# The K stage in pairs of d_ff tiles, its 64 remaining channels as two row tiles of TensorE

## The chip, the cores and the metric

The kernel runs on one core of a Trainium2 chip. The time is the device time of one execution in microseconds (us); lower is better. The granted TensorE clock was 0.998 to 1.0 in every profiled run, and every run quoted here is recorded as fast (none shows the lower clock and longer time of a slow run).

## The reference, cut to what matters

A causal convolution over 7 positions runs along the sequence, and its output goes through a channel mix. B = 8 batches, S = 4160 positions, D = 192 channels, d_ff = 1024.

```python
xk = mu_k * x + (1.0 - mu_k) * x_prev
xr = mu_r * x + (1.0 - mu_r) * x_prev
k = np.maximum(xk @ w_k, 0.0)          # K: 192 -> 1024
v = k * k @ w_v                        # V: 1024 -> 192
r = 1.0 / (1.0 + np.exp(-(xr @ w_r)))  # R: 192 -> 192
return (r * v).astype(np.float32)
```

192 channels are 128 and 64: the full height of TensorE's array of 128 rows, and half of it. The change is about that half.

## The kernel before: the parts that matter

Two batches are worked on together. For a step of 512 positions, `xk[:, 0, :]` and `xk[:, 1, :]` hold the 128 high channels of the two batches, and `xk[:, 2, :]` their 64 low channels, one batch on partitions 0 to 63 and the other on 64 to 127. The low matmul uses all 128 rows with weights of which one half is zeros.

```python
    def load_w(w, src):
        nc.gpsimd.dma_start(out=w[:, 0, :], in_=src[0:P, :])
        nc.gpsimd.dma_start(out=w[0:LO, 1, :], in_=src[P:D, :])
        nc.gpsimd.dma_start(out=w[LO:P, 2, :], in_=src[P:D, :])
        nc.gpsimd.memset(w[LO:P, 1, :], 0.0)
        nc.gpsimd.memset(w[0:LO, 2, :], 0.0)

    def load_rest():
        load_w(wr, moe_w_r)
        nc.gpsimd.dma_start(out=wv, in_=moe_w_v.rearrange("(f p) d -> p f d", p=P))
    # ... cut ...
    def k_mm(n):                      # one slot: one tile f of 128 d_ff channels
        # ... cut ...
            for i in range(2):        # L308
                nc.tensor.matmul(
                    out=ps[:, i, :], lhsT=wk[:, 0, fs], rhs=xk[:, i, :], start=True, stop=False
                )
            for i in range(2):        # L312
                nc.tensor.matmul(
                    out=ps[:, i, :], lhsT=wk[:, 1 + i, fs], rhs=xk[:, 2, :], start=False, stop=True
                )
```

The schedule is written by hand, slot by slot. A slot issues one K tile, then what a table has for it: R and V matmuls of an earlier step, and for later steps a convolution head (`conv_mm`) or a group of six transposes (`tr_mm`). ScalarE takes the Relu, the sigmoid and copies of the convolution (`conv_out`); VectorE takes squares, mixes, the product with R and the copies of the transposes (`tr_out`).

```python
            for h in range(H):
                at(pe, c0 + h, conv_mm, p, g, h)      # c0 = n0 - 22: eight slots in a row
                # ... cut: conv_out one slot later ...
            for j in range((nb + 1) // 2):
                at(pe, r0 + j, tr_mm, p, g, j)        # r0 = n0 - 13: five slots in a row
                at(dve, r0 + 1 + j, tr_out, p, g, j)
    # ... cut ...
        for n in range(-60, NSLOT + LAG_V + 3):
            run(early, n)
            if 0 <= n < NSLOT:
                k_mm(n)
            run(act, n)
            run(pe, n)
            if 0 <= n < NSLOT:
                k_relu(n)
            run(dve, n)
            if 1 <= n <= NSLOT:
                k_square(n - 1)
```

Three pools of PSUM, the memory that the matmuls write, hold two buffers each: for K (`psK`), for V, and one (`psM`) that convolution, transposes and R share in turn. A matmul into `psM` therefore waits until the tile before the last one has been copied out.

## Time and profile before

| | before |
|---|---|
| time, median of 4 runs (range) | 523.50 us (523.03 to 525.36) |
| span of the profiled run | 519.7 us |
| busy: TensorE, VectorE, ScalarE | 95%, 82%, 73% |
| TensorE's share of the chain that ended last | 92% |
| K matmul of 512 columns, start to start | 216 ns |

The prediction below shows the lines. Busy time counts records that overlap on TensorE, so the cost of a matmul is the distance between two starts, not its mean duration. The chain says which engine sets the end: here TensorE, in all its stages. The profiled run took 521.39 us, less than each of the four timed ones; e9 below has the likely cause, the start.

### The profile page before, as it was taken

The numbers are of one execution on the slowest core, as the hardware profiler recorded it, in microseconds if no ns is written. First come the engines' busy times: TensorE is split into PE (matmuls) and PEld (weight loads), VectorE is DVE, ScalarE is ACT, GpSimd is POOL, SyncE is SP. The second block draws the span as 40 slices with busy tenths as digits, with TensorE's granted clock in tenths as the row PEclk, the third lists the DMA queues.
The fourth block names the chain that finished last, engine by engine and source line by source line (L and its number), as shares of the span: only waits on it lengthen the run. The fifth ranks groups of instructions, "written<-read, shape, count | busy, mean of one in ns | idle before, by whom it ended". The sixth has DMA issues, their size and how long they took to land.

```text
span 519.7 us, 10640 instructions
## 1 busy us (share of the span) xinstructions
PE 492.5 (95%) x4256; PEld 360.1 (69%) x4256; DVE 425.3 (82%) x676; ACT 380.0 (73%) x545; POOL 51.9 (10%) x74
## 2 busy tenths in 40 slices
PE   0597999999999999999999999999999999999996
PEld 0345777777777777777777777777777777777776
DVE  1498897979889797997889799797898979798862
ACT  3278768687787868778686877868687786867772
POOL 9532100001020000101002010100100000000000
PEclk9999999999999999999999999999999999999999
DMA  9986451818136181714517171451711111121113
GB/s 126 171 94 85 72 106 47 130 47 129 48 71 113 47 130 47 115 62 74 101 62 115 55 115 62 76 101 52 123 47 62 56 47 62 47 62 62 49 58 100
DMA packets 76625, 41.92 MB, mean 81 GB/s; under 512 B 42912, under 2 KB 76192, under 8 KB 76576
## 3 DMA queue, kind: packets, MB, share of 16 engines
q0 software_dynamic: 39184, 15.15, 25.7%
q1 hardware_dynamic: 37392, 26.10, 16.6%
q8 instruction: 33, 0.54, 0.4%
q14 instruction: 16, 0.13, 0.1%
HBM read 30.56 MB, written 25.82 MB: 108 GB/s over the span
## 4 chain that ended last, share of the span: by engine, by line
PE 92%; DMA 3%; DVE 2%; ACT 2%; issue 0%; DVEq 0%; SPq 0%
PE ps_v L388 33%; PE ps_k L308 21%; PE ps_k L312 21%; PE ps_c L193 4%; PE ps_t L226 4%; PE ps_r L370 4%; PE ps_r L369 4%; ACT k_sb L339 1%; DMA w_scr<-w_row 1%; DMA toe<-w_scr 1%; DVE yT L237 1%; DMA w_raw<-in_weight_dram 1%; DVE xk L275 1%; DVE d L253 0%; PE ps_k L326 0%
## 5 line engine op out<-in xcount | busy, mean ns | idle before, releaser
L339 ACT ACTIVATE k_sb<-ps_k 128x1024 bf16<-128x1024 f32 x260 | 266.6, 1025 | 108.2 <-PE ps_k L312 105.8
L388 PE MATMUL ps_v<-wv,k 128*128 128x192 bf16 x2048 | 210.9, 246 | 0.0
L388 PEld LDWEIGHTS <-k 128*128 128x128 bf16 x2048 | 173.5, 98 | 35.6 <-issue 2.2
L353 DVE TENSOR_TENSOR k<-k_sb 128x1024 bf16<-128x1024 bf16 x256 | 175.0, 684 | 24.2 <-ACT k_sb L339 22.6
L308 PE MATMUL ps_k<-xk,wk 128*128 128x512 bf16 x512 | 153.1, 381 | 1.8 <-DVE xk L275 1.4
L312 PE MATMUL ps_k<-xk,wk 128*128 128x512 bf16 x512 | 153.2, 381 | 0.0
L400 DVE TENSOR_TENSOR o_sb<-ps_v,r_sb 128x384 f32<-128x384 f32 x132 | 72.4, 548 | 39.6 <-PE ps_v L388 35.6
L312 PEld LDWEIGHTS <-wk 128*128 128x128 bf16 x512 | 50.3, 98 | 61.1 <-issue 0.8
L378 ACT ACTIVATE r_sb<-ps_r 128x384 bf16<-128x384 f32 x132 | 65.0, 492 | 8.1 <-PE ps_r L370 5.0
L275 DVE SCALAR_TENSOR_TENSOR xk<-d,mu,yT 128x1024 bf16<-128x1024 bf16 x64 | 65.5, 1024 | 0.6
L193 PE MATMUL ps_c<-xb,toe 128*116 128x432 bf16 (+2 forms) x136 | 46.6, 346 | 20.0 <-DMA toe<-w_scr 16.4
L275 DVE SCALAR_TENSOR_TENSOR xr<-d,mu,yT 128x1024 bf16<-128x1024 bf16 x64 | 64.7, 1015 | 0.9
L369 PE MATMUL ps_r<-wr,xr 128*128 128x192 bf16 x256 | 63.0, 246 | 0.6 <-ACT y L213 0.6
L370 PE MATMUL ps_r<-wr,xr 128*128 128x192 bf16 x256 | 63.0, 246 | 0.0
L210 ACT CAST y<-ps_c 116x432 bf16<-116x432 f32 (+4 forms) x99 | 45.5, 460 | 16.3 <-PE ps_c L193 16.0
L87 POOL DMA_DIRECT2D xb<-in_x_dram x34 | 32.2, 950 | 247.3 <-PE ps_c L193 218.4
L308 PEld LDWEIGHTS <-wk 128*128 128x128 bf16 x512 | 46.4, 98 | 3.9 <-issue 2.9
L226 PEld LDWEIGHTS <-y 116*128 116x128 bf16 x432 | 30.1, 99 | 20.4 <-issue 1.2
L237 DVE COPY yT<-ps_t 128x696 bf16<-128x696 bf16 (+1 forms) x80 | 38.3, 479 | 4.7 <-PE ps_t L226 3.8
L193 PEld LDWEIGHTS <-toe 128*116 128x116 bf16 x136 | 18.6, 138 | 32.4 <-DMA toe<-w_scr 16.4
L226 PE MATMUL ps_t<-ident,y 116*128 116x116 bf16 x432 | 35.9, 217 | 0.5 <-DVE yT L221 0.3
L253 DVE TENSOR_TENSOR d<-yT 128x1536 bf16<-128x1536 bf16 (+1 forms) x36 | 32.0, 889 | 0.1
(55 smaller groups left out, 135.9 us busy)
## 6 DMA issues: line engine op xcount, KB each, us to landing
out_dram<-o_sb SPq DMA_DIRECT2D x128, 192.0 KB, 2.0
xb<-in_x_dram POOLq DMA_DIRECT2D x23, 432.0 KB, 7.7
xb<-in_x_dram POOLq DMA_DIRECT2D x7, 384.0 KB, 5.7
xb<-in_x_dram POOLq DMA_DIRECT2D x4, 192.0 KB, 4.6
wv<-in_moe_w_v_dram POOLq DMA_DIRECT2D x1, 384.0 KB, 6.5
out_dram<-o_sb SPq DMA_DIRECT2D x8, 48.0 KB, 2.0
xb<-in_x_dram POOLq DMA_DIRECT2D x8, 45.8 KB, 3.8
wk<-in_moe_w_k_dram POOLq DMA_DIRECT2D x1, 256.0 KB, 5.5
```

Of the source, the lines that this page charges most:

```text
L193: nc.tensor.matmul(out=ps[:BLK, :nb], lhsT=toe[:, h, :], rhs=xbs[p, g][:, :nb, :, h * G : (h + 1) * G], start=True, stop=True,)
L226: nc.tensor.transpose(out=ps[:, c, i, :], in_=ys[p, g][:BLK, 2 * j + i, c * P : (c + 1) * P], identity=ident[:BLK, :BLK],)
L275: nc.vector.scalar_tensor_tensor(out=o, in0=d[r0:r1, sl, :L], scalar=mu[r0:r1, i, part : part + 1], in1=yT[r0:r1, sl, c0 : c0 + L], op0=AL ...
L308: nc.tensor.matmul(out=ps[:, i, :], lhsT=wk[:, 0, fs], rhs=xk[:, i, :], start=True, stop=False)
L312: nc.tensor.matmul(out=ps[:, i, :], lhsT=wk[:, 1 + i, fs], rhs=xk[:, 2, :], start=False, stop=True)
L339: nc.scalar.activation(out=k_sb, in_=ps.rearrange("p a b -> p (a b)"), func=AF.Relu)
L353: nc.vector.tensor_tensor(out=o, in0=k_sb, in1=k_sb, op=ALU.mult)
L369: nc.tensor.matmul(out=o, lhsT=hi, rhs=wr[:, 0, :], start=True, stop=False)
L370: nc.tensor.matmul(out=o, lhsT=lo, rhs=wlo, start=False, stop=True)
L378: nc.scalar.activation(out=r_sb[:, :n, :], in_=ps[:, :n, :], func=AF.Sigmoid)
L388: nc.tensor.matmul(out=o, lhsT=k2[:, f, t * P : (t + 1) * P], rhs=wv[:, f, :], start=(f == 0), stop=(f == NF - 1),)
L400: nc.vector.tensor_tensor(out=o_sb[:, :n, :], in0=v_ps.pop(m)[:, :n, :], in1=r_sbs.pop(m)[:, :n, :], op=ALU.mult)
```

## The change

The intent: the two low matmuls need 64 rows each. Given as two tiles of 64 rows, they can run side by side in the time of one. Going between 128-row and 64-row mode costs something, so two d_ff tiles are taken together in the order high, low, low, high. That makes two changes of mode per pair, one per tile. The diff, cut to its core:

```diff
-    wk = const.tile([P, 4, DF], BF16)
+    wk = const.tile([P, 2, DF], BF16)
@@ load_w
-        nc.gpsimd.dma_start(out=w[LO:P, 2, :], in_=src[P:D, :])
-        nc.gpsimd.memset(w[LO:P, 1, :], 0.0)
-        nc.gpsimd.memset(w[0:LO, 2, :], 0.0)
+        nc.gpsimd.dma_start(out=w[LO:P, 1, :], in_=src[P:D, :])
@@ load_rest, before V's weights are asked for
+        nc.gpsimd.memset(wr[:, 2:4, :], 0.0)
+        nc.gpsimd.tensor_copy(out=wr[0:LO, 2, :], in_=wr[0:LO, 1, :])
+        nc.gpsimd.tensor_copy(out=wr[LO:P, 3, :], in_=wr[LO:P, 1, :])
@@ k_mm
+        first = f % 2 == 0
+        def hi():
             for i in range(2):
                 nc.tensor.matmul(
-                    out=ps[:, i, :], lhsT=wk[:, 0, fs], rhs=xk[:, i, :], start=True, stop=False
+                    out=ps[:, i, :], lhsT=wk[:, 0, fs], rhs=xk[:, i, :], start=first, stop=not first
                 )
+        def lo():
             for i in range(2):
+                r = slice(i * LO, (i + 1) * LO)
                 nc.tensor.matmul(
-                    out=ps[:, i, :], lhsT=wk[:, 1 + i, fs], rhs=xk[:, 2, :], start=False, stop=True
+                    out=ps[:, i, :], lhsT=wk[r, 1, fs], rhs=xk[r, 2, :], start=not first, stop=first
                 )
+        for part in (hi, lo) if first else (lo, hi):
+            part()
@@ schedule: slots in pairs, both K tiles first
+            for n in real:
+                k_mm(n)
+            for n in ns:
+                run(act, n)
+                run(pe, n)
+                # ... cut: Relu, VectorE's work and the square, slot by slot, as before ...
```

More of the change, by code (lines that the diff above doesn't have):

```diff
@@ L165, in load_w @@
         nc.gpsimd.dma_start(out=w[0:LO, 1, :], in_=src[P:D, :])
-        nc.gpsimd.dma_start(out=w[LO:P, 2, :], in_=src[P:D, :])
-        nc.gpsimd.memset(w[LO:P, 1, :], 0.0)
-        nc.gpsimd.memset(w[0:LO, 2, :], 0.0)
+        nc.gpsimd.dma_start(out=w[LO:P, 1, :], in_=src[P:D, :])
     def load_rest():
         load_w(wr, moe_w_r)
+        nc.gpsimd.memset(wr[:, 2:4, :], 0.0)
+        nc.gpsimd.tensor_copy(out=wr[0:LO, 2, :], in_=wr[0:LO, 1, :])
+        nc.gpsimd.tensor_copy(out=wr[LO:P, 3, :], in_=wr[LO:P, 1, :])
         nc.gpsimd.dma_start(out=wv, in_=moe_w_v.rearrange("(f p) d -> p f d", p=P))
-    def fill_tails():
-        for w in (wk, wr):
-            nc.gpsimd.tensor_copy(out=w[0:LO, 3, :], in_=w[0:LO, 1, :])
-            nc.gpsimd.tensor_copy(out=w[LO:P, 3, :], in_=w[LO:P, 2, :])
         for t in tails:
@@ L302, in k_mm @@
         p, s, f = where(n)
-        xk = xks.get((p, s))
-        if s < NSTEP:
-            ps = psK.tile([P, 2, STEP], FP32, tag="k", name="ps_k")
-            fs = slice(f * P, (f + 1) * P)
+        if s == NSTEP:
+            return k_mm_tail(n)
+        xk = xks[p, s]
+        ps = psK.tile([P, 2, STEP], FP32, tag="k", name="ps_k")
+        k_ps[n] = ps
+        fs = slice(f * P, (f + 1) * P)
+        first = f % 2 == 0
+        def hi():
             for i in range(2):
                 nc.tensor.matmul(
-                    out=ps[:, i, :], lhsT=wk[:, 0, fs], rhs=xk[:, i, :], start=True, stop=False
+                    out=ps[:, i, :], lhsT=wk[:, 0, fs], rhs=xk[:, i, :], start=first, stop=not first
@@ L310, in k_mm @@
                 )
+        def lo():
             for i in range(2):
+                r = slice(i * LO, (i + 1) * LO)
                 nc.tensor.matmul(
-                    out=ps[:, i, :], lhsT=wk[:, 1 + i, fs], rhs=xk[:, 2, :], start=False, stop=True
+                    out=ps[:, i, :], lhsT=wk[r, 1, fs], rhs=xk[r, 2, :], start=not first, stop=first
                 )
-        else:
-            ps = psK.tile([P, NF, 2 * TAIL], FP32, tag="k", name="ps_k")
-            for f in range(NF):
-                fs = slice(f * P, (f + 1) * P)
-                nc.tensor.matmul(
-                    out=ps[:, f, :],
-                    lhsT=wk[:, 0, fs],
-                    rhs=tails[p % 2][:, 0, 1, :],
-                    start=True,
-                    stop=False,
-                )
-                nc.tensor.matmul(
-                    out=ps[:, f, :],
-                    lhsT=wk[:, 3, fs],
-                    rhs=tails[p % 2][:, 0, 0, :],
-                    start=False,
-                    stop=True,
-                )
@@ L333, in k_mm, with k_mm_tail @@
-        k_ps[n] = ps
+        for part in (hi, lo) if first else (lo, hi):
+            part()
+    def k_mm_tail(n):
+        p, s, f = where(n)
+        ps = psK.tile([P, NF, 2 * TAIL], FP32, tag="k", name="ps_k")
+        k_ps[n] = ps
+        for f in range(NF):
+            fs = slice(f * P, (f + 1) * P)
+            nc.tensor.matmul(
+                out=ps[:, f, :],
+                lhsT=wk[:, 0, fs],
+                rhs=tails[p % 2][:, 0, 1, :],
+                start=True,
+                stop=False,
+            )
+            nc.tensor.matmul(
+                out=ps[:, f, :],
+                lhsT=wk[:, 1, fs],
+                rhs=tails[p % 2][:, 0, 0, :],
+                start=False,
+                stop=True,
+            )
@@ L365, in r_mm @@
             st, c = t // 4, (t % 4) * P
-            hi, lo, wlo = xr[:, st, c : c + P], xr[:, 2, c : c + P], wr[:, 1 + st, :]
+            hi, lo, wlo = xr[:, st, c : c + P], xr[:, 2, c : c + P], wr[:, 2 + st, :]
         else:
-            hi, lo, wlo = tails[p % 2][:, 1, 1, :], tails[p % 2][:, 1, 0, :], wr[:, 3, :]
+            hi, lo, wlo = tails[p % 2][:, 1, 1, :], tails[p % 2][:, 1, 0, :], wr[:, 1, :]
         nc.tensor.matmul(out=o, lhsT=hi, rhs=wr[:, 0, :], start=True, stop=False)
@@ L421 @@
     at(early, -16, load_rest)
-    at(early, 4, fill_tails)
     for p in range(NPAIR):
@@ L457, in run, with slots @@
             fn(*a)
-    with tc.manual_schedule():
-        for n in range(-60, NSLOT + LAG_V + 3):
-            run(early, n)
-            if 0 <= n < NSLOT:
-                k_mm(n)
-            run(act, n)
-            run(pe, n)
-            if 0 <= n < NSLOT:
-                k_relu(n)
-            run(dve, n)
-            if 1 <= n <= NSLOT:
-                k_square(n - 1)
+    def slots():
+        n = -60
+        while n < NSLOT + LAG_V + 3:
+            two_ = 0 <= n < NSLOT and where(n)[1] < NSTEP
+            yield (n, n + 1) if two_ else (n,)
+            n += 2 if two_ else 1
+    with tc.manual_schedule():
+        for ns in slots():
+            for n in ns:
+                run(early, n)
+            real = [n for n in ns if 0 <= n < NSLOT]
+            for n in real:
+                k_mm(n)
+            for n in ns:
+                run(act, n)
+                run(pe, n)
+                if n in real:
+                    k_relu(n)
+                run(dve, n)
+                if 1 <= n <= NSLOT:
+                    k_square(n - 1)
 _INS = ['x', 'weight', 'moe_mu_k', 'moe_mu_r', 'moe_w_k', 'moe_w_v', 'moe_w_r']
```

## The prediction

> **What bounds the kernel now.** I read first the page's table of engines, then the chain that ended last, then the costliest groups. The first column after an engine's name is busy microseconds, then the share of the 519.7 us span, then instructions.
>
> ```profile
> PE 492.5 (95%) x4256; PEld 360.1 (69%) x4256; DVE 425.3 (82%) x676; ACT 380.0 (73%) x545; POOL 51.9 (10%) x74
> ...
> PE 92%; DMA 3%; DVE 2%; ACT 2%; issue 0%; DVEq 0%; SPq 0%
> PE ps_v L388 33%; PE ps_k L308 21%; PE ps_k L312 21%; PE ps_c L193 4%; PE ps_t L226 4%; PE ps_r L370 4%; PE ps_r L369 4%; ACT k_sb L339 1%; DMA w_scr<-w_row 1%; DMA toe<-w_scr 1%; DVE yT L237 1%; DMA w_raw<-in_weight_dram 1%; DVE xk L275 1%; DVE d L253 0%; PE ps_k L326 0%
> ```
>
> TensorE is 92% of the chain. L308 (the 128 high channels, one matmul per batch) and L312 (the 64 low channels of both batches, stacked on 128 rows against weights half of which are zeros) have 21% each. The change attacks L312.
>
> ```profile
> L388 PE MATMUL ps_v<-wv,k 128*128 128x192 bf16 x2048 | 210.9, 246 | 0.0
> L353 DVE TENSOR_TENSOR k<-k_sb 128x1024 bf16<-128x1024 bf16 x256 | 175.0, 684 | 24.2 <-ACT k_sb L339 22.6
> L308 PE MATMUL ps_k<-xk,wk 128*128 128x512 bf16 x512 | 153.1, 381 | 1.8 <-DVE xk L275 1.4
> L312 PE MATMUL ps_k<-xk,wk 128*128 128x512 bf16 x512 | 153.2, 381 | 0.0
> ```
>
> The mean duration, 381 ns, is not the price of a matmul, because they are pipelined; the price is the distance between starts. That is read from the timeline (start, length, engine, line), here one slot, that is one tile of 128 d_ff channels, with its share of the V, R and convolution work:
>
> ```profile
> 199.84 0.59 PE L308 MATMUL ps_k<-xk,wk 128*128 128x512 bf16 x2
> ...
> 200.06 0.31 PEld L312 LDWEIGHTS <-wk 128*128 128x128 bf16 x2
> 200.27 0.59 PE L312 MATMUL ps_k<-xk,wk 128*128 128x512 bf16 x2
> ...
> 200.71 0.35 PE L193 MATMUL ps_c<-xb,toe 128*116 128x432 bf16 x1
> ...
> 200.89 0.82 PE L388 MATMUL ps_v<-wv,k 128*128 128x192 bf16 x8
> ...
> 201.55 0.25 PE L369 MATMUL ps_r<-wr,xr 128*128 128x192 bf16 x1
> ...
> 201.63 0.25 PE L370 MATMUL ps_r<-wr,xr 128*128 128x192 bf16 x1
> ...
> 201.71 0.59 PE L308 MATMUL ps_k<-xk,wk 128*128 128x512 bf16 x2
> ```
>
> From start to start: L308 0.43 us for two, L312 0.44 for two, convolution 0.18, eight V matmuls 0.66, two R 0.16. The sum is 1.87 us, exactly the slot, so TensorE never waits. Weight loads cost nothing: L312's begin at 200.06, while L308 still streams. A slot with six transposes instead of a convolution takes 2.00 us (63.68 to 65.68). The table of waits agrees: TensorE waits 16.4 us for the first Toeplitz weights, and after that 5.5 us in all.
>
> **What the Trainium skill says.**
> (1) "TensorE: Matmul & The Clock Gate", "Measured speedup vs the span model": a pack of row tiles takes one matmul's duration plus about 4 ns per further tile. The trace before has no row tile, so this is untested here.
> (2) "TensorEngine Tiling (Array Packing)", "Key Properties": "Changing tiling mode (not just tile) drains the TensorE". No duration is given. The built program before has one mode only (128 rows), so the trace can't say. This is the number that decides.
> (3) First page again, "Single matmul latency": (398 + N)/2.4 ns at full clock, N columns. For 512 columns that is 379 ns; the trace has 381. So the tail after a matmul's last column is about 166 ns, the most that a drain by itself should cost. The part "What happens when you issue a matmul" gives the passage through the array alone as about 128 cycles, 53 ns at 2.4 GHz: the least.
> (4) Same page, "What overlaps and what doesn't": matmuls stay in order and weight loads are pulled ahead. The trace agrees for one mode (200.06 above). Whether a load is pulled ahead over a change of mode, neither says. If it isn't, its 98 ns come on top.
>
> **The change part by part.**
> Removed: L312's two matmuls no longer run one after the other. Each reads 64 rows, the first rows 0 to 63 and the second rows 64 to 127, and they write different PSUM banks. Two of 213 ns become one of 213 plus 4, a saving of 209 ns per tile. In the built program I counted 256 matmuls and 256 weight loads at each of the two row positions, so all 256 full tiles take part. Instruction and weight-load counts don't change.
> Added: changes of mode. The order in a pair is high(n), low(n), low(n+1), high(n+1): two changes per pair, 256 in all, s ns each.
> Net per tile 209 - s. Where does it count? In the first ten slots there is no V work, and ScalarE sets the pace: a slot then takes 1.34 us (L308 starts at 36.53 and 37.87) although TensorE's own work is only 0.87 + 0.18. So I count 246 tiles, and the ideal is 246 x 0.209 = 51 us.
> My choice of s: 110 ns, an estimate, half way between the bare passage through the array (53) and the full tail (166). It gives 246 x 0.099 = 24 us. Other values: s = 53 gives 38 us; 166 gives 11; 166 plus an exposed weight load of 98 gives 264, a loss of 14 us.
> Moved: the pair issues both K tiles, then the V, R and convolution work of both slots. Two K tiles fill both psK buffers at once, and the shared psM buffers (two, for convolution, transposes and R) turn over in half the distance. ScalarE, in start-to-start times: Relu 0.93, copy 0.40, sigmoid 0.42, so a convolution pair needs 2 x 0.93 + 2 x 0.40 + 0.42 = 3.1 us of a pair's new 2 x (1.87 - 0.10) = 3.5. A copy queues behind the first Relu and lets go of its buffer just about when the second convolution wants it: hardly a wait.
> VectorE is tighter. A step of eight slots needs eight squares (0.684), four V products (0.554), mixes (1.30 + 1.28 + 0.75 + 0.75), one difference (0.97), and 2.5 transpose copies (0.516): 14.0 us by record. Records overlap by about 0.08 us each (the product at 199.88 lasts 0.56, the square begins at 200.35), and there are 19.5 of them, so about 12.5 us of a step that takes 15 to 16 now and 14.5 after: some 86%. Mixes and transpose copies fall into the same slots, and a pair that has two transpose copies, two mixes, a product and two squares needs about 4.6 us against 3.7 of TensorE. The debt is paid in the next pair, where the last transposes may wait for a psM buffer. I allow 0.35 us for each of some 14 groups of 16 slots: 5 us given back.
> Off the path: the Pool engine loses two memsets of 0.95 us and two copies of 64x1024 (1.06, 1.69), but now waits for R's weights to land (some 4 us) before it issues V's weights and the next x. Those were issued at 11.98 and 12.90; even 5 us later they are there (6.5 and 7.7 us to landing) well before V starts at about 43 and those blocks' convolution at about 30. Worth zero.
> Sum: 523.6 - 24 + 5 = 504.6. The parallel pairing was presumably tuned, that is, someone chose one change per tile because a change costs something but less than it saves; that pulls me slightly down, to 502.
>
> **The rivals.**
> A: the drain plus exposed weight loads eat the gain (s near or over 209). For it: "drains", and no overlap of loads over a mode change is promised. Against it: the tail of 166 ns alone is still under 209. It makes 520 to 538.
> B: the change of mode is nearly free (s about 50), and then VectorE and the psM buffers become the bound. For it: VectorE's 82% busy now. Then 38 us are saved and some 8 given back: 493; with s near zero, about 483.
> C: row tiles don't really run side by side, because each one's weight load stands between them. For it: the program alternates load, matmul, load, matmul. Against: loads are pulled ahead in the trace. It would make 523.6 plus 246 x s, about 550.
> D: the wait moves to psK: low(n+1) waits for the Relu of tile n-1. Against it: that Relu can start as soon as the previous pair's K work is over, and V, R and convolution work of two slots, 2 x 1.0 us, lie between.
>
> **Range and chances.** Chances on s: about 25% near 50 (485 to 495), 35% near 110 (498 to 508), 22% near 166 (511 to 518), 18% at 210 or more, C included (520 and up). The limits of 2% are 513.1 and 534.1. Faster by over 2%: 0.66; within: 0.24; slower: 0.10. Predicted 502, eight times in ten from 482 to 528.
>
> **What would show it.** In the timeline of a pair, the two low matmuls of a tile start within some 5 ns of each other, and low(n) to low(n+1) is about 217 ns: the packing is right. The distance from the last high(n) start to the first low(n) start, less 213, is s, and likewise at the second change; 110 expected. The weight loads there show whether they wait for the drain. A V stage still of 0.66 us for eight says nothing else moved. TensorE's waits on transpose copies (DVE) and on y copies (ACT), 2.2 and about 1 us now, should grow to about 5 together; 15 or more would make B's second half right. The prediction fails if s lies outside 50 to 210, or if the pairing itself costs more than the row tiles win.

## The result, and the profile after

| | before | after |
|---|---|---|
| time, median of 4 runs each | 523.50 us | 503.94 us |
| range | 523.03 to 525.36 | 503.74 to 504.73 |
| span of the profiled run | 519.7 us | 502.3 us |
| first to last V matmul, start to start | 471.5 us | 455.1 us |

The ratio is 0.9623 (95% interval 0.9597 to 0.9648). Ratios in this document are the mean time of one kernel's fast runs over that of the other's fast runs of the same rounds, so they aren't quite the ratio of the medians.

The stretch from the first to the last V matmul is worked out from the records of each trace. It leaves out the start of the kernel, which varies from run to run (below), and serves from here on as the measure of what TensorE does. Its edges differ a little: kernels that take K tiles in pairs have 244 full tiles in it and the others 245, which is 0.9 us, and e6, e8, e11 and e12 have 107 convolution matmuls in it in place of 111, which is 0.7 us.

The page after, engines, chain and the two K groups:

```profile
PE 459.3 (91%) x4193; PEld 312.9 (62%) x4256; DVE 420.6 (84%) x676; ACT 375.6 (75%) x545; POOL 45.9 (9%) x69
...
PE 75%; DVE 12%; issue 5%; ACT 3%; DMA 3%; DVEq 0%; SPq 0%
...
L311 PE MATMUL ps_k<-xk,wk 128*128 128x512 bf16 x449 | 140.9, 384 | 1.1 <-DVE xk L271 0.3
...
L318 PE MATMUL ps_k<-xk,wk 64*128 64x512 bf16 x512 | 78.5, 383 | 8.5 <-ACT k_sb L350 0.9
```

L318 is the low part: as many matmuls as before, of about the same length each, in 78.5 us instead of 153.2. That is what two at a time looks like in the busy column. The 63 matmuls that are fewer on the page are all L311's; 512 are in the program, so these are records missing from the trace. And VectorE, 2% of the chain before, is now 12%.

The timeline of one pair's K work and what follows, after:

```profile
204.50 0.18 PEld L311 LDWEIGHTS <-wk 128*128 128x128 bf16 x2
204.58 0.59 PE L311 MATMUL ps_k<-xk,wk 128*128 128x512 bf16 x2
...
205.11 0.11 PEld L318 LDWEIGHTS <-wk 64*128 64x128 bf16 x4 [0.42 <-issue]
205.11 0.61 PE L318 MATMUL ps_k<-xk,wk 64*128 64x512 bf16 x4
...
205.64 0.11 PEld L311 LDWEIGHTS <-wk 128*128 128x128 bf16 x2 [0.42 <-issue]
205.65 0.60 PE L311 MATMUL ps_k<-xk,wk 128*128 128x512 bf16 x2
...
206.09 0.82 PE L399 MATMUL ps_v<-wv,k 128*128 128x192 bf16 x8
```

Four low matmuls and a change of mode take 205.65 - 205.11 = 0.54 us. Weight loads no longer run ahead here: the low ones begin at 205.11, with the first low matmul, where before they began in the middle of the high ones.

The single records give it to the nanosecond. Distances from start to start, in an ordinary stretch of this trace (medians of all such steps):

```
high -> high (same mode)              216
high -> low   (mode changes)          312   = 216 + 96
low  -> low   (other row tile)          4
low  -> low   (next pair of matmuls)  223
low  -> low   (other row tile)          4
low  -> high  (mode changes back)     308   = 216 + 92
high -> high  (the first after it)    226   = 216 + 10
```

From the first high start of a pair to its next piece of work this is 216 + 312 + 4 + 223 + 4 + 308 + 226 + 216 = 1509 ns. Before it was 8 x 216 = 1728. The gain is 219 ns per pair, and with 122 pairs in the V stretch 26.7 us.

But the stretch is only 471.5 - 455.1 = 16.4 us shorter, and 0.9 of that is the tile at its edge. TensorE's part of the table of waits, before (us in total, times, longest):

```profile
PE ps_c L193 <- DMA toe<-w_scr: 16.4, 1, 16.4
PE ps_c L193 <- DVE yT L237: 2.2, 4, 0.8
```

and after:

```profile
PE ps_c L189 <- DMA toe<-w_scr: 15.8, 1, 15.8
PE ps_t L222 <- DVE yT L233: 7.6, 14, 0.6
PE ps_c L189 <- DVE yT L233: 2.8, 4, 1.6
```

`yT` is what VectorE copies the transposes to. One of the 14 new waits, TensorE's timeline after:

```profile
96.33 0.47 PE L222 MATMUL ps_t<-ident,y 116*128 116x116 bf16 x6
...
97.38 0.25 PE L381 MATMUL ps_r<-wr,xr 128*128 128x192 bf16 x1
98.28 0.31 PE L222 MATMUL ps_t<-ident,y 116*128 116x116 bf16 x3 [0.65 <-DVE yT L233]
```

and VectorE's, the same time:

```profile
95.42 0.52 DVE L233 COPY yT<-ps_t 128x696 bf16<-128x696 bf16 x1
95.97 0.75 DVE L271 SCALAR_TENSOR_TENSOR xr<-d,mu,yT 128x512 bf16<-128x512 bf16 x1
96.64 0.55 DVE L411 TENSOR_TENSOR o_sb<-ps_v,r_sb 128x384 f32<-128x384 f32 x1
97.11 0.68 DVE L364 TENSOR_TENSOR k<-k_sb 128x1024 bf16<-128x1024 bf16 x1
97.71 0.52 DVE L233 COPY yT<-ps_t 128x696 bf16<-128x696 bf16 x1
```

The transposes of 96.33 are done at about 96.8, but VectorE works without a gap and copies them at 97.71, after a copy, a mix, a product and a square. The last transposes of the group need that buffer and start at 98.28, 0.90 us after the matmul before them, where 0.08 is usual. By starts, such steps from R to transposes lose 10.2 us in 15 cases, 0.3 to 0.8 us each (the table of waits says 7.6, because a matmul's record goes on for some 0.17 us after TensorE is free for the next). With 0.9 us more at the few steps from transposes to convolution and the tile at the edge, the balance is 471.5 - 26.7 - 0.9 + 10.2 + 0.9 = 455.0, against 455.1 measured.

### The profile page after: what moved, and what is told of

It reads as the page before. It is cut to its first block, busy times and chain, and to the rows that moved or that the text cites. A ratio compares the mean times of both kernels' runs of the same rounds, so it can differ in the third digit from the quotient of the medians.

```text
span 502.3 us, 10506 instructions
## 1 busy us (share of the span) xinstructions
PE 459.3 (91%) x4193; PEld 312.9 (62%) x4256; DVE 420.6 (84%) x676; ACT 375.6 (75%) x545; POOL 45.9 (9%) x69
## 4 chain that ended last, share of the span: by engine, by line
PE 75%; DVE 12%; issue 5%; ACT 3%; DMA 3%; DVEq 0%; SPq 0%
PE ps_v L399 29%; PE ps_k L311 19%; PE ps_k L318 12%; PE ps_c L189 4%; DVE yT L233 4%; PE ps_r L381 4%; PE ps_r L380 4%; DVE xr L271 3%; PE ps_t L222 3%; DVE k L364 3%; ACT k_sb L350 2%; DMA w_scr<-w_row 1%; DVE xk L271 1%; DVE o_sb L411 1%; DMA w_raw<-in_weight_dram 1%
## 5 line engine op out<-in xcount | busy, mean ns | idle before, releaser
L350 ACT ACTIVATE k_sb<-ps_k 128x1024 bf16<-128x1024 f32 x260 | 260.1, 1025 | 37.0 <-PE ps_k L318 35.1
L364 DVE TENSOR_TENSOR k<-k_sb 128x1024 bf16<-128x1024 bf16 x256 | 175.1, 685 | 13.2 <-ACT k_sb L350 13.1
L311 PE MATMUL ps_k<-xk,wk 128*128 128x512 bf16 x449 | 140.9, 384 | 1.1 <-DVE xk L271 0.3
L318 PE MATMUL ps_k<-xk,wk 64*128 64x512 bf16 x512 | 78.5, 383 | 8.5 <-ACT k_sb L350 0.9
L311 PEld LDWEIGHTS <-wk 128*128 128x128 bf16 x512 | 37.8, 98 | 56.0 <-issue 55.7
L206 ACT CAST y<-ps_c 116x432 bf16<-116x432 f32 (+4 forms) x99 | 46.3, 468 | 17.9 <-PE ps_c L189 17.4
L318 PEld LDWEIGHTS <-wk 64*128 64x128 bf16 x512 | 15.1, 94 | 56.5 <-issue 56.5
```

Of the source, the lines that this page charges most:

```text
L311: nc.tensor.matmul(out=ps[:, i, :], lhsT=wk[:, 0, fs], rhs=xk[:, i, :], start=first, stop=not first)
L318: nc.tensor.matmul(out=ps[:, i, :], lhsT=wk[r, 1, fs], rhs=xk[r, 2, :], start=not first, stop=first)
L350: nc.scalar.activation(out=k_sb, in_=ps.rearrange("p a b -> p (a b)"), func=AF.Relu)
L364: nc.vector.tensor_tensor(out=o, in0=k_sb, in1=k_sb, op=ALU.mult)
```

## The experiments

All outputs are right. "V stretch" is the measure of above. Each time is a median of 4 runs (6 for e9); the time of the kernel before in the same rounds stands beside it.

**e1: the pairing alone.** The kernel before with the pairs and the order high, low, low, high; full 128-row matmuls with zeros, no mode change.

```diff
-        for n in range(-60, NSLOT + LAG_V + 3): ...
+        for ns in slots(): ...           # as in the change
-            high(start=True); low(stop=True)
+            (high, low) if f % 2 == 0 else (low, high)
```

> The kernel before, with the pairing alone: two d_ff tiles issued together in the order high, low, low, high, all matmuls on 128 rows, no change of mode. Theory (the pairing by itself costs little, since each pair keeps its old length and the vector engine has time for the transpose copies): 525 us, 523 to 528, with 1 to 4 us of new waits of transposes on their copies. Rival (it is the bunching of the pair that gives back some 6 us, whatever the pair's length): 529 or more.

Measured: 532.76 us (529.83 to 535.53) against 523.47; ratio 1.0179 (1.0124 to 1.0235). V stretch 478.2, 6.7 more than before, 7.6 with the tile at the edge. The rival is right. Steps from R to transposes lose 6.9 us in 12 cases. TensorE's waits in e1:

```profile
PE ps_c L193 <- DMA toe<-w_scr: 19.3, 1, 19.3
PE ps_t L226 <- DVE yT L237: 4.7, 11, 0.4
PE ps_c L193 <- DVE yT L237: 2.8, 4, 1.6
```

The pairing by itself makes transposes wait for their copies, even with pairs of the old length; the rest of the loss is a start that came 2.9 us later (first line; see e9).

**e2: row tiles without pairs**, so two changes of mode per tile.

```diff
-        first = f % 2 == 0
+        first = True
-            two_ = 0 <= n < NSLOT and where(n)[1] < NSTEP
+            two_ = False
```

> Row tiles without pairs: every tile by itself, high then low, so the mode changes twice per tile. Theory (a change costs 105 ns, packing saves 209 per tile): per tile 209 - 210, so 523 us, 520 to 526, no gain at all over the kernel before. Rival (a change costs less than its gap in the timeline, part of it being hidden or being caused by the pair): 510 to 517.

Measured: 522.60 us against 523.47; ratio 0.9986 (0.9949 to 1.0024). As the theory had it: packing that needs two changes per tile gains nothing. In the V stretch, 474.2, it even loses 2.7 us; the total is even because the start was earlier (e9). A tile in its timeline:

```profile
205.34 0.39 PE L318 MATMUL ps_k<-xk,wk 64*128 64x512 bf16 x2
205.66 0.39 PE L189 MATMUL ps_c<-xb,toe 128*116 128x432 bf16 x1
205.89 0.82 PE L399 MATMUL ps_v<-wv,k 128*128 128x192 bf16 x8
```

The two low matmuls and the change take 0.32 us. The convolution after the change takes 0.23 where it took 0.18 before: by starts, leaving the mode costs 100 ns here and another 45 in the next step. No run tells what these 45 ns are.

**e3: pairs with two changes per tile** (high, low, high, low).

```diff
-        first = f % 2 == 0
+        first = True
```

> The changed kernel, pairs kept, but each tile in the order high, low, so four changes of mode per pair in place of two. Theory (105 ns each): 256 more changes, some 246 of them on the path, add 26 us, of which 3 to 5 come back because a longer pair leaves the vector engine more time: 526 us, 522 to 531. Rival (only the first change in a pair is dear): 510 to 515.

Measured: 529.14 us against 523.47; ratio 1.0112 (1.0067 to 1.0156). That is 25.2 more than the changed kernel. V stretch 479.1, 24.0 more, of which by starts 27.6 are the 244 changes that were added, and the transposes' loss falls from 10.2 to 7.0. So a change costs 27.6/244 = 113 ns on the path, its aftermath included, whichever it is, and a longer pair gives VectorE some time back.

**e4: transposes one group per pair**, the rest as changed.

```diff
-                at(pe, r0 + j, tr_mm, p, g, j)
+                rj = r0 + j if late or n0 == 0 else n0 - 14 + 2 * j
+                at(pe, rj, tr_mm, p, g, j)
```

> The changed kernel with the transpose groups one per pair (every other slot) in place of one per slot, nothing else. Theory (the last transposes of each group wait about 0.5 us for a copy that the vector engine is late with, 10 us in all, because two groups, two mixes, a product and two squares fall into one pair): these waits vanish and the time is 497 us, 495 to 500. Rival (the vector engine is simply near its limit, so the wait turns up at another place): 502 to 504.

Measured: 499.83 us against 523.47; ratio 0.9552 (0.9515 to 0.9589). V stretch 450.2, 4.8 less than the changed kernel. The waits at the last transposes are gone, but at 3 places, where a group's last transposes now share a slot with the next group's first convolution, that convolution waits, 3.7 us in all. The gain is 4 us where 7 were expected.

**e5: the same spread in the kernel before**, as a control.

> The kernel before with the same spread of the transposes as in e4, without pairs or row tiles. Theory (before, TensorE waited for hardly any copy after the start): the same as before, 523.5 us within 1.5. Rival (the spread is a gain of its own and has nothing to do with the change): 517 to 520.

Measured: 526.53 us against 521.74; ratio 1.0076 (1.0006 to 1.0146); V stretch 474.4. The spread is no gain of its own; it even costs 3.0 us of the V stretch, at the same places as in e4 (three steps, 3.1 us). The expected "same" was missed by that and by a late start (e9).

**e6: convolution heads also one per pair.**

```diff
+            far = not late and n0 > 0        # then c0 = n0 - 30
-                at(pe, c0 + h, conv_mm, p, g, h)
+                at(pe, c0 + (2 * h if far else h), conv_mm, p, g, h)
```

> The changed kernel with both the transpose groups and the convolution heads one per pair. Theory (the convolution slots cause no wait of TensorE in the trace): no more than 1 us better than e4, 496 to 498 us. Rival (copies by the scalar engine let go of the shared buffers late): 493 or less.

Measured: 524.08 us against 521.74; ratio 1.0025 (0.9976 to 1.0075); V stretch 472.3. A clear miss of both theories. Both kinds of work now fell into the even slot of the same pair, the transposes first: steps from transposes to convolution lose 24.0 us in 24 cases. VectorE's busy time is nearly that of e4 (422.8 us, 420.2 there). It is the place, not the amount, that decides.

**e7: the low matmuls of equal rows one after the other**: rows 0 to 63 of both tiles, then rows 64 to 127 of both.

```diff
-        hi(n); lo(n, 0); lo(n, 1); lo(n+1, 0); lo(n+1, 1); hi(n+1)
+        hi(n); lo(n, 0); lo(n+1, 0); lo(n, 1); lo(n+1, 1); hi(n+1)
```

> The changed kernel with the four low matmuls of a pair in another order: both on rows 0 to 63 first, then both on rows 64 to 127, so that only the middle two can run side by side. Theory (matmuls start in order, and two on the same rows run one after the other): the low part of a pair takes three streams of 213 ns in place of two, 123 pairs on the path, 26 us more less some 4 us of waits that vanish: 526 us, 522 to 530. Rival (the order doesn't matter, the gain comes from fewer rows or cheaper loads): 503 to 506.

Measured: 511.68 us against 521.74; ratio 0.9793 (0.9745 to 0.9841). V stretch 462.2, 7.1 more than the changed kernel, not 22. The low block, e7:

```profile
201.04 0.61 PE L318 MATMUL ps_k<-xk,wk 64*128 64x512 bf16 x4
201.59 0.61 PE L311 MATMUL ps_k<-xk,wk 128*128 128x512 bf16 x2
```

0.55 us, as in the changed kernel (0.54): four low matmuls in two streams, although the program names equal rows in succession. The starts lie 7, 219 and 7 ns apart. A record doesn't say which rows a matmul used, but its semaphores tell which matmul it is. In the built program the second of the four waits for a psK buffer, and the third, the first tile's matmul on rows 64 to 127, signals the Relu. In the trace the matmul that signals starts second, in 125 of 128 blocks, and the one that waits starts third. So the third was started ahead of its turn, beside the first on the other rows, and the theory's strict order of starts is wrong. Its signal still comes late: 625 ns after the block begins (median), when the waiting matmul has ended too; in the changed kernel it comes after 409. That is the cause of the 7.1 us: the Relu of the first tile starts 0.65 us after the low block begins (201.69; in the changed kernel 0.43, at 205.54 after 205.11). The copy of the first convolution stands behind that Relu, and the second convolution waits for it: 48 steps from R to convolution lose 142 ns (median) each, 7.0 us in all.

**e8: convolution in the even, transposes in the odd slot of a pair.**

```diff
-                rj = ... n0 - 14 + 2 * j      (e6)
+                rj = ... n0 - 13 + 2 * j
```

> The changed kernel with one convolution head per pair, always in its even slot, and one transpose group per pair, always in its odd slot. In e6 both stood in the even slot, transposes first, so convolution and R of the same pair waited for a copy just asked for (24 us of waits on transpose copies). Theory (the 10 us given back are waits for copies that have less than one slot to be made; here each has most of a pair): the waits vanish, 503.9 - 10 = 494 us, 492 to 497. Rival (the vector engine is near its limit, so the debt shows at another place): 500 or more.

Measured: 507.80 us against 522.03; ratio 0.9711 (0.9653 to 0.9769). V stretch 456.6, 1.6 more than the changed kernel. The number was missed, and the cause was in the edit: a batch pair has 65 slots, so slots ahead of its first one have the other parity. There a convolution follows the transposes of the previous group at once: 15 steps lose 12.1 us. e11 mends it.

**e9: the kernel before with the changed kernel's order at the start.** Pool fills R's tail weights, and so waits for R's weights to land, before it asks for V's weights and the next x.

```diff
         load_w(wr, moe_w_r)
+        nc.gpsimd.tensor_copy(out=wr[0:LO, 3, :], in_=wr[0:LO, 1, :])
+        nc.gpsimd.tensor_copy(out=wr[LO:P, 3, :], in_=wr[LO:P, 2, :])
         nc.gpsimd.dma_start(out=wv, ...)
```

> The kernel before, with only the order of the Pool engine's work at the start as in the changed kernel: it fills R's tail weights, and so waits for R's weights to land, before it asks for V's weights and the next x. Theory (in the kernel before, V's weights and x, asked for at 12 to 15 us, run beside the Toeplitz load at 12.2 and delay it by 1 to 4 us, differently in each run): the Toeplitz load lands in some 3.4 us in place of 4.2 to 7.2, the start is earlier and the times scatter less: 521 us, 520 to 522, within 1 us. Rival (chance of the runs): 523.5 with a scatter of 4 us, as before.

Measured: 521.13 us (6 runs, 520.59 to 522.46) against 522.03 (11 runs, 520.31 to 527.91); ratio 0.9971 (0.9918 to 1.0024). Within the noise of the mean, but the scatter falls from 7.6 to 1.9 us. The other kernels say the same: all eleven with the changed order, e9 included, stay within 2.0 us each, those with the old one scatter by 2.3 to 7.6. The V stretch is that of the kernel before, 471.5. Pool's timeline at the start, before:

```profile
11.98 0.93 POOL L172 DMA_DIRECT2D wv<-in_moe_w_v_dram  x1
12.90 2.01 POOL L87 DMA_DIRECT2D xb<-in_x_dram  x2
```

and in the changed kernel:

```profile
14.82 0.34 POOL L171 COPY wr<-wr 64x192 bf16<-64x192 bf16 x1 [4.92 <-DMA wr<-in_moe_w_r_dram]
15.22 0.35 POOL L172 COPY wr<-wr 64x192 bf16<-64x192 bf16 x1
15.51 0.93 POOL L173 DMA_DIRECT2D wv<-in_moe_w_v_dram  x1
```

The Toeplitz weights (`toe`, the convolution's weights laid out as a matrix), for which the first convolution waits, are asked for at 12.15. In the profiles of the kernels that ask for V's weights at 12.0 they land 4.2 (before), 7.2 (e1) and 6.5 us (e5) after that; in e9 and in every profile with the changed order 3.3 to 3.5. So with the small reordering these weights land some 1 to 4 us earlier, differently in each run. Whether V's weights or the x behind them delay the load, no run tells.

**e10: R's mixes later**, TensorE's order as changed.

```diff
-                at(dve, n0 + ((-3, -2, -1, -1)[j] if late else j - 5), mix, p, s, i, part)
+                when = (-3, -2, -1, -1)[j] if late else (-5, -4, 1, 2)[j]
+                at(dve, n0 + when, mix, p, s, i, part)
```

> The changed kernel with the two mixes for R of each step moved six and four slots later, out of the pairs that have two transpose groups; TensorE's order is untouched. Theory (the vector engine's debt, 2.0 us of it these mixes, makes the last transposes of a group wait 0.8 us for the copy): 14 waits of 0.8 us shrink to under 0.2, 496 us, 494 to 499. Rival (the wait comes from the pair order by itself, the copy's place behind a square that waits for its Relu): 502 to 504.

Measured: 501.14 us against 522.03; ratio 0.9583 (0.9526 to 0.9640). V stretch 451.5, 3.6 less than the changed kernel; the transposes' loss goes from 10.2 to 6.4 us, still in 14 cases. The mixes are about a third of the cause. The rest stays when they are gone; that it is the copy's place behind a product and a square fits e4 and e11, but this run alone doesn't show it.

**e11: e8 mended**, each kind of work in its own slot of the pair everywhere.

```diff
+            def own(n):
+                return n if n >= p * SPP else n - 1
-                ch = c0 + 2 * h
+                ch = own(c0 + 2 * h)
-                rj = n0 - 13 + 2 * j
+                rj = own(n0 - 13 + 2 * j)
```

> e8 mended. Its slots were counted from the next batch pair's first slot, and a batch pair has 65 slots, so before a boundary even and odd were exchanged and a convolution head came straight after the previous group's transposes: 15 waits of 0.8 us, 12 us in all. Here each head and each transpose group keeps to its own slot of the pair everywhere. Theory (what was given back are waits for copies with less than a slot to be made): nearly no wait left between the first and last V matmul, that stretch 10 us shorter than in the changed kernel, 494 us, 492 to 497. Rival (the vector engine is near its limit, so the debt shows elsewhere): 500 or more.

Measured: 492.87 us (492.38 to 493.41) against 522.19; ratio 0.9426 (0.9385 to 0.9466). V stretch 441.9, 13.1 less than the changed kernel (12.4 without the convolutions at the edge). Its engines and chain:

```profile
PE 464.5 (95%) x4256; PEld 314.3 (64%) x4256; DVE 421.3 (86%) x676; ACT 378.7 (77%) x545; POOL 45.9 (9%) x69
...
PE 91%; DMA 5%; ACT 3%; issue 0%; DVE 0%; POOL 0%; DVEq 0%; ACTq 0%; SPq 0%
```

VectorE has its highest share of busy time (86%), and 0% of the chain, after 12%. Between the first and the last V matmul only the mode changes still lose time: no other kind of step loses as much as 0.4 us in total against the kernel before. This version beats both kernels.

**e12: e11 with e10's later mixes.**

> e11 with the later mixes of e10 as well. Theory (with the copies off TensorE's path the vector engine's load doesn't matter any more): within 1 us of e11. Rival (its load still delays a copy or a square here and there): 2 us or more better than e11.

Measured: 494.46 us against 522.19; ratio 0.9461 (0.9410 to 0.9512); V stretch 442.9. No gain: the rival is wrong. It is even 1.6 us slower than e11 in the same rounds (493.96 to 495.90 against 492.38 to 493.41), more than the theory's 1 us; 1.0 us of it is lost in steps from K to convolution. With the copies off TensorE's path, later mixes no longer help.

## Why the prediction was right, point by point

The time came to 503.94 us; 502 was predicted, from 482 to 528. The terms of the sum:

- **What bounds it: right.** TensorE's order of work set the time before, and e11 shows that it still can after.
- **Packing, 209 ns per tile: right.** Two row tiles start 4 ns apart, and the second two follow after 223 ns. Rival C is refuted.
- **A change of mode, 110 ns chosen: right, slightly high.** It costs 96 ns into the row tiles, and 92 plus 10 out of them. e2 and e3 bear out the size where changes are added: 113 ns with all that follows. Rival A, the drain with an exposed weight load at 264 ns, is refuted, though the loads do wait for the change, as the trace's weight loads at 205.11 show. By the records' starts 92 of the 96 ns go by before the first load of the new mode begins, and its matmul starts 4 ns after that load; how much of the load is hidden, no run tells.
- **Net gain, 24 us: 26.7 by starts.** 122 pairs lie in the V stretch, so 244 tiles where the prediction counted 246.
- **Given back, 5 us: right in place, too small by half, and the cause only in part.** The wait came at the predicted place, the last transposes of a group, as often as predicted (14 of 15 cases; one is at the start), but at 0.68 us on average in place of 0.35: 10.2 us. The prediction's own sign lies between its marks: the waits on transpose copies and on y copies grew to about 12 us, where it had put 5, and 15 for rival B. The prediction charged the wait to VectorE's debt from mixes and copies. e10 shows that the mixes are a third of it; e1 shows that the pair's order makes the wait even when no time is saved; e4, e6 and e11 show that the place of copy and matmul decides. Rival B's second half was thus nearer than its first: the change of mode isn't free, but the shared buffers do take 10.2 of the 26.7 us.
- **The ScalarE copies, "hardly a wait": right, but close.** e7 moves a Relu by 0.22 us and loses 7.0 us there.
- **The start, worth zero: wrong by a little.** The later request for V's weights lets the Toeplitz weights land sooner, in 3.4 us after 4.2 to 7.2. e9 narrows the scatter from 7.6 to 1.9 us; by how much it lowers the time is within the noise.
- **Rival D, a wait for psK: refuted.** TensorE waits 0.9 us for a Relu in the whole run.

That the sum came so close is partly luck, because errors offset each other: about 6 us too little given back (10.2 and 0.9, against 5), against 3 us more saved (26.7) and about 3 us outside the V stretch, where the prediction had put nothing. Of these last, 1.0 us is there in the profiled runs; the other 2 us are the difference between the gain of the medians (19.6) and that of the profiled spans (17.4), with what e9 shows as its likely cause. The last step, from 504.6 down to 502 on a guess about how the change was tuned, had no measurement behind it and led away from the 503.94 measured.

## What to carry to other kernels

Two half-height matmuls side by side save a whole stream, but only if the mode changes seldom: here a stream of 216 ns is paid for with 99 ns per change, so one change per saved stream gains and two gain nothing. Grouping work to save changes bunches it, and bunched matmuls ask for a shared PSUM buffer sooner than the copy can be made. After grouping, look at the table of waits by buffer, and place the work so that each user of the buffer has most of a group's time to be copied out: in e11 that was worth another 11 us, though VectorE's busy share rose.

## What the Trainium skill lacked or had wrong

- "TensorEngine Tiling (Array Packing)", "Key Properties", says that a change of tiling mode drains TensorE, and gives no time. Here 96 ns go by into 64-row tiles and 92 plus 10 ns out of them, each time after matmuls of 512 columns; out of them into a convolution, 100 plus 45 ns.
- Neither that page nor "TensorE: Matmul & The Clock Gate" says whether weight loads are pulled ahead over a change of mode. In one mode loads run ahead (200.06 in the trace before). Over a change they don't: they begin with the first matmul of the new mode (205.11), and the loads of high matmuls wait in the same way (205.64).
- "TensorE: Matmul & The Clock Gate", "What overlaps and what doesn't", has matmuls in strict order of start. With both matmuls of equal rows named first (e7) the four still took two streams, 7, 219 and 7 ns apart, and the third in the program started second, in 125 of 128 blocks. So the order of starts isn't strict between row tiles. The order of signals was kept: the third's came 625 ns after the block began, after 409 in the changed kernel.
- The same page, "Back-to-back issue gap", gives about 131 ns per matmul of 512 columns in a sustained stream with weight loads. Here it is 216 ns throughout, which is the same section's formula for the isolated gap, 512/2.4 + 2.5 ns.
